# Product 5 by inner products in both chunks of the last gated layer, product 6 in the last one

## The chip, the cores and the metric

The kernel runs on one core of a Trainium2 chip. The metric is the device time of one execution in microseconds, given as the median of repeated runs. A profile of one further execution belongs to it. In the profile PE is TensorE (the matmuls), PEld its loading of weights, DVE VectorE, ACT ScalarE, POOL GpSimd and SP SyncE; here SP issues nearly all transfers.

## The reference

Four layers with residuals, A, B, A, B, on x of 2048 tokens by D = 1024, with F = 3584:

```python
x = x + A(layernorm(x));  x = x + B(layernorm(x))
x = x + A(layernorm(x));  x = x + B(layernorm(x))

def A(x):   # linear attention, 32 heads of 32
    q, k, v = heads(x @ wqkv)
    pq, pk = phi(q), phi(k)          # t + 1 if t > 0 else exp(t), + 1e-6
    kv = einsum("bhsd,bhse->bhde", pk, v);  z = pk summed over s
    return heads_joined((pq @ kv) / (pq . z + 1e-6)) @ wo

def B(x):   # gated, with ReLU
    gate, up = x @ W_gate, x @ W_up          # 1024 x 3584 each
    return (relu(gate) * up) @ W_down
```

The layers are called 0 to 3; layers 1 and 3 are gated. The change lies in these: product 5 and product 6 below are parts of `x @ W_gate` and `x @ W_up`.

## The kernel before

A gated layer works on two chunks c of 1024 tokens; (3, 1) is the second chunk of layer 3. In a chunk `glu` runs over 14 units u of 256 columns of F. In a unit gate ("g") and up ("u") are each a product of 1024 tokens x 1024 by 1024 x 256, cut into 2 x 2 blocks and multiplied by Strassen's scheme in Winograd's form: seven products m = 1 to 7. Each product is one group of four matmuls, 128 x 128 weights by 512 tokens, so a plain unit has 14 groups. The weights come from a ring of tiles. A tile of the ring holds, for one matrix and one unit, the raw weights and four sums of weight blocks, called T; product 5 uses T[0], product 7 T[1], product 6 T[2] and product 4 T[3]. The sums are made in (1, 0), stored in DRAM (`tgu`), and loaded with the raw weights from then on (`load_gu`: two transfers of 512 KB for each matrix and unit). The token side has its own sums s1 to s4, made once for each chunk.

The result of product 5 is V. In a unit the groups follow one another as 5, 1 for g and u, then 2, 6 for g and u, then 7, 3 and 4. An eviction copies X (product 1) to Y on ACT, Z = Y + V is made on VectorE (`zg`, `zu`, line 1300), V = Y + V after product 7 (line 1320), and `put` multiplies by the ReLU of the gate on VectorE (line 1275) into h. TensorE's groups of a unit are all at line 1259.

In (3, 1), from u = 2 on, product 5 is not computed in the unit. For two units together (a pair: the same token blocks, both matrices, two units of weights) it is made by a second level of the same scheme: `inner_gi` has seven steps (five, one, two, six, seven, three, four), each one group of four matmuls of 256 columns (line 1094), in two PSUM banks of their own. The steps run in the odd unit before the pair, each after one of the unit's groups; after which is written by hand in `INNER_AT`, counted in groups. The results are 128 x 512 tiles laid in memory that x has left (`gi_v`), two pairs deep. The weight side of the inner products is made in (3, 0): `make_gi` loads T[0] of four units again from DRAM, makes four sums for each pair on VectorE (line 1072), and stores seven blocks of each pair in DRAM (`gi`); `load_gi` brings the seven blocks of a pair to (3, 1). Because of this, `load_gu` leaves out T[0] of these units.

What sets the order: every engine runs its instructions in the order of issue. `later.at(n, f)` issues f after n more groups of TensorE; `behind(self.last_put, ...)` places work on VectorE after the last `put`. SP's queue carries loads of the ring, of the pairs, the stores of sums, the transposes of activations, and rows of x that are sent to DRAM (`send_away`) and brought back (`bring_back`), because the memory is full. `make_dd` makes and stores the sums of one product of `down`, which follows the 14 units of a chunk. A ring tile can be loaded again when the unit that used it is done; the ring is five tiles deep, and layer_B asks for the tiles up to five ahead at a unit's start. A tile of "big" (16 slots) is also the home of h, of the ring, and of scratch.

Of the kernel before, what the change touches and what calls it, by code (L numbers as in the profile page):

```python
# [8 lines left out]
ALU = mybir.AluOpType  # L9
# [3 lines left out]
F16 = mybir.dt.float16  # L13
PSUM = bass.MemoryType.PSUM
P = 128
# [77 lines left out]
class _Net:  # L93
    def __init__(self, tc, ctx, x_d, wqkv_d, wo_d, wg_d, wu_d, wd_d, out_d):
# [36 lines left out]
        self.dd = {p: self.spill.tile([P, 7, self.U // 2, NW // 2], F16, name=f"dd{p}") for p in self.DEEP}  # L131
        self.gi = [self.spill.tile([P, 7, 2, 2, P], F16, name=f"gi{p}") for p in range(self.U // 2)]
        self.later = _Later()
# [838 lines left out]
    def plan_B(self, l):  # L972
        for c in range(2):
            for u in range(self.U):
                for w in "gu":
                    self.ring.add((l, c, w, u), lambda t, w=w, u=u, first=(l == 1 and c == 0),
                                  lo=(l, c) == (3, 1) and u > 1: self.load_gu(t, w, u, first, lo))
# [70 lines left out]

    GI_AT = (0, 3, 5), (1, 4, 2, 6)

    def make_gi(self, pairs, at):

        def load():
            t = self.slot(f"gi{pairs[0]}", [P, 2, 2, 2, 4, P], F16)
            for i, p in enumerate(pairs):
                for a in range(2):
                    for n, w in enumerate("gu"):
                        self.nc.sync.dma_start(out=t[:, i, n, a, :, :].rearrange("p k f -> p (k f)"),
                                               in_=self.tgu[w, 2 * p + a][:, 0, :])
            self.gi_b = [[[t[:, i, :, a, 2 * j:2 * j + 2, :] for a in range(2)] for j in range(2)]  # L1060
                         for i in range(2)]
            self.later.at(4, lambda: [store(i, m, self.gi_b[i][j][a]) for i in range(2)
                                      for m, j, a in ((0, 0, 0), (3, 1, 0), (5, 1, 1))])

        def store(i, m, b):
            for n in range(2):
                self.nc.sync.dma_start(out=self.gi[pairs[i]][:, m, n, :, :], in_=b[:, n, :, :])

        def sums(i, n):
            (b11, b12), (b21, b22) = self.gi_b[i]  # L1070
            out, a, b, m = ((b11, b12, b11, 1), (b12, b22, b12, 4), (b22, b22, b11, 2), (b21, b21, b22, 6))[n]
            self.nc.vector.tensor_tensor(out=out, in0=a, in1=b, op=ALU.subtract)
            self.later.at(2, lambda: store(i, m, out))

        self.later.at(at, load)
        for i in range(2):
            for n in range(4):
                self.later.at(at + 12 + 2 * (4 * i + n), lambda i=i, n=n: self.behind(
                    self.last_put, lambda n: sums(i, n), (n,)))

    def inner_gi(self, p):

        nc, v = self.nc, self.nc.vector
        H, V, A = NW // 2, self.gi_v[p % 2], self.gi_a
        B = {m: self.gi_w[:, n] for n, m in enumerate((1, 5, 6, 2, 7, 3, 4))}
        out = lambda i, a: V[:, a, :, i, :]
# [3 lines left out]

        def mm(m, b, start=False):
            for w in range(2):
                for k in range(2):
                    nc.tensor.matmul(b[:, w, :], lhsT=B[m][:, w, k, :], rhs=A[m][:, k, :],
                                     start=start and w == 0 and k == 0, stop=k == 1, skip_group_check=True)

        def five():
            z = bank(0)
            mm(5, z, True)
            copy(out(1, 1), z)  # L1100

# [9 lines left out]
        def six():  # L1111
            mm(6, S["y"])
            S["z"] = bank(0)
            v.tensor_tensor(out=S["z"], in0=S["y"], in1=out(1, 1), op=ALU.add)

        def seven():
            mm(7, S["y"])
            v.tensor_tensor(out=out(1, 1), in0=S["y"], in1=out(1, 1), op=ALU.add)

# [9 lines left out]

    def ready_gi(self):  # L1130

        flat = lambda t: self.xall[:, t:t + 2, :].rearrange("p a n -> p (a n)")
        H = NW // 2
        self.gi_w = flat(0).bitcast(F16)[:, 0:28 * P].rearrange("p (m w k f) -> p m w k f", m=7, w=2, f=P)
        self.gi_v = [flat(t).rearrange("p (a w i n) -> p a w i n", a=2, w=2, n=H) for t in (2, 4)]
        S1, S2, S3, S4 = (self.x[6].bitcast(F16)[:, n * NW:(n + 1) * NW].rearrange("p (k n) -> p k n", n=H)
                          for n in range(4))
        s1 = self.xs[3, 1][0]
        (a11, a12), (a21, a22) = ([s1[:, 2 * j:2 * j + 2, i * H:(i + 1) * H] for j in range(2)] for i in range(2))
        v = self.nc.vector  # L1140
        v.tensor_tensor(out=S1, in0=a21, in1=a22, op=ALU.add)
        v.tensor_tensor(out=S2, in0=S1, in1=a11, op=ALU.subtract)
        v.tensor_tensor(out=S3, in0=a11, in1=a21, op=ALU.subtract)
        v.tensor_tensor(out=S4, in0=a12, in1=S2, op=ALU.subtract)
        self.gi_a = {1: a11, 2: a12, 3: S4, 4: a22, 5: S1, 6: S2, 7: S3}

    def load_gi(self, p):
        self.nc.sync.dma_start(out=self.gi_w, in_=self.gi[p])

    def raw_gu(self, t):  # L1150
# [4 lines left out]

    def load_gu(self, t, w, u, first, lo):
        self.nc.sync.dma_start(out=self.raw_gu(t),
                               in_=self.wgu_v[w][:, :, u * 2 * P:(u + 1) * 2 * P])
        if not first:
            self.nc.sync.dma_start(out=t[:, 4 + lo:8, :].bitcast(F16), in_=self.tgu[w, u][:, lo:4, :])  # L1160

# [79 lines left out]

    INNER_AT = (0, 2, 3, 5, 7, 9, 11)

    def glu(self, l, c, u, hT):
# [12 lines left out]
        def mm(w, m, ps, start=False):  # L1257
            for k in range(4):
                nc.tensor.matmul(ps, lhsT=W[w][m][:, k, :], rhs=A[m][:, k, :],  # L1259
                                 start=start and k == 0, stop=k == 3, skip_group_check=True)  # L1260
            if inner and next(turn) in self.INNER_AT:
                inner.pop(0)()
            later.tick()

        deep = (l, c) == (3, 1)
        inner = self.inner_gi(u // 2 + 1) if deep and u % 2 and u + 1 < self.U else []
        turn = count(0 if u > 1 else -2)
        h = hT[u // 2][:, (u % 2) * 4:(u % 2) * 4 + 4, :]
# [14 lines left out]
        def one(w):  # L1283
            X[w] = self.ps.tile([P, NW], F32, tag="a", name=f"x{w}")
            mm(w, 1, X[w], True)
            Y[w] = self.ps3.tile([P, NW], F32, tag="b", name=f"y{w}")
            nc.scalar.activation(out=Y[w], in_=X[w], func=ACT.Copy)

# [8 lines left out]
        def six(w):  # L1297
            mm(w, 6, Y[w])
            Z[w] = self.ps.tile([P, NW], F32, tag="a", name=f"z{w}")
            self.last_z = nc.vector.tensor_tensor(out=Z[w], in0=Y[w], in1=V[w], op=ALU.add)  # L1300

        if c == 0 and u == 0:
            for f in (one, two, five, six):
                for w in "gu":
                    f(w)
        elif deep and u > 1:
            for k, w in enumerate("gu"):
                V[w] = self.gi_v[u // 2 % 2][:, u % 2, k, :, :].rearrange("p i n -> p (i n)")
            for f in ((one,), (two, six)):
# [8 lines left out]
        for w in "gu":  # L1318
            mm(w, 7, Y[w])
            nc.vector.tensor_tensor(out=V[w], in0=Y[w], in1=V[w], op=ALU.add)  # L1320
            if w == "g":
# [17 lines left out]
    def down(self, l, c, hT, final):  # L1339
# [214 lines left out]
        else:  # L1554
            product("T3", raw(2), Y, False, third_done)
            product("T4", raw(3), Y, False, last_done)

    def layer_B(self, l, final):
        ring = self.ring
# [5 lines left out]
        for c in range(2):  # L1565
# [3 lines left out]
            for u in range(self.U):  # L1569
# [26 lines left out]
                if (l, c) == (3, 0) and u in (3, 7, 9):  # L1596
                    self.make_gi({3: (1, 2), 7: (3, 4), 9: (5, 6)}[u], 1)
                if (l, c, u) == (3, 1, 0):
                    self.later.at(4, lambda: behind(self.last_put, self.ready_gi))
                if (l, c) == (3, 1) and u % 2 == 0 and u + 2 < self.U:  # L1600
                    self.later.at(5 if u == 0 else 1, lambda u=u: self.load_gi(u // 2 + 1))
                if (l, c, u) in ((1, 1, 6), (3, 0, 4)):
                    self.make_dd("T4" if l == 1 else "21", 1)
# [76 lines left out]
```

## Time and profile before

| | us |
|---|---|
| median of 3 runs | 1445.16 |
| lowest and highest | 1445.1 and 1445.32 |
| the profiled execution's own time | 1445.22 |
| its span, first to last instruction | 1443.4 |
| TensorE busy in the span | 1436.3 |
| VectorE, ACT, POOL busy | 980.0, 615.7, 308.7 |

The span is what the trace shows; about 1.8 us of the execution's time lie around it. A busy matmul row counts overlapping instructions, so the time from one start to the next start tells what a matmul costs, not its length. Where the stages lie in the span (us): units of (1, 1) from 479.1 to 646.4, of (3, 0) from 930.9 to 1112.4, of (3, 1) from 1194 to 1360.4.

### The profile page before, as it was taken

How to read it: one execution, taken by the hardware profiler on the slowest of the kernel's cores; microseconds unless marked ns; L12 is line 12 of the kernel's file. 1: busy time of each engine (PE TensorE's matmuls, PEld its weight loads, DVE VectorE, ACT ScalarE, POOL GpSimd, SP SyncE). 2: the span in 40 equal slices, each digit the busy share in tenths (PEclk: the TensorE clock that was granted, in tenths of full speed). 3: DMA queues.
4: the chain of work that ended last, by engine and by line, in shares of the span. 5: the costliest groups of instructions: out<-in, count | busy, mean ns of one | idle time of the engine just before them, and what ended most of it. 6: DMA issues, size and time to landing. Idle time of an engine off the chain costs nothing.

```text
span 1443.4 us, 20611 instructions
## 1 busy us (share of the span) xinstructions
PE 1436.3 (100%) x7502; PEld 716.7 (50%) x7502; DVE 980.0 (68%) x1839; ACT 615.7 (43%) x1119; POOL 308.7 (21%) x221
## 2 busy tenths in 40 slices
PE   9999999999999999999999999999999999999998
PEld 4444444444455444445654444444444565555457
DVE  7978698677594456539778885765555864444695
ACT  7872564233334234332068626633333433444300
POOL 1453861011100011110031576410111011111102
PEclk9999999999999999999999999999999999999999
DMA  9950787898469999646983119978976698655465
GB/s 285 240 161 8 175 212 203 287 328 264 164 202 299 352 300 311 201 134 208 292 268 95 59 30 256 266 229 248 306 242 215 213 308 260 206 183 175 153 235 181
DMA packets 345253, 315.93 MB, mean 219 GB/s; under 512 B 109280, under 2 KB 307424, under 8 KB 344128
## 3 DMA queue, kind: packets, MB, share of 16 engines
q1 hardware_dynamic: 337104, 293.32, 68.3%
q10 hardware_dynamic: 6560, 17.24, 3.2%
q0 software_dynamic: 1488, 4.07, 0.8%
q8 instruction: 58, 0.95, 0.3%
q14 instruction: 43, 0.35, 0.1%
HBM read 232.78 MB, written 57.15 MB: 201 GB/s over the span
## 4 chain that ended last, share of the span: by engine, by line
PE 94%; DVE 4%; ACT 1%; issue 1%; DVEq 0%; ACTq 0%
PE ps L495 11%; PE yu L1259 10%; PE yg L1259 10%; PE dy L1384 8%; PE xg L1259 6%; PE xu L1259 6%; PE dx L1384 6%; PE ps L778 4%; PE zu L1259 3%; PE zg L1259 3%; PE my L577 3%; PE vu L1259 3%; PE vg L1259 3%; PE dyT L1436 2%; PE mv L577 2%; PE mx L577 2%
## 5 line engine op out<-in xcount | busy, mean ns | idle before, releaser
L1259 PEld LDWEIGHTS <-w 128*128 128x128 f16 (+1 forms) x3040 | 297.3, 98 | 352.6 <-issue 3.9
L1324 POOL TENSOR_TENSOR h<-m5u,m5g 128x512 f16<-128x512 f32 x44 | 56.6, 1286 | 594.7 <-DVE m5u L1320 555.5
L495 PE MATMUL ps<-w,xnT 128*128 128x512 bf16 x768 | 170.0, 379 | 0.2 <-DVE pq L441 0.2
L1300 DVE TENSOR_TENSOR zg<-yg,m5g 128x512 f32<-128x512 f32 x44 | 30.7, 699 | 130.7 <-PE yg L1259 126.8
L495 PEld LDWEIGHTS <-xnT 128*128 128x128 bf16 x768 | 74.4, 98 | 90.0 <-issue 1.8
L1259 PE MATMUL yu<-s,w 128*128 128x512 f16 x448 | 114.9, 379 | 0.6 <-DVE zu L1300 0.5
L1259 PE MATMUL xu<-xnT,w 128*128 128x512 f16 x448 | 115.0, 379 | 0.0
L1259 PE MATMUL xg<-xnT,w 128*128 128x512 f16 x448 | 114.9, 379 | 0.0
L1259 PE MATMUL yg<-s,w 128*128 128x512 f16 x448 | 114.9, 379 | 0.0
L1384 PEld LDWEIGHTS <-h 128*128 128x128 f16 x672 | 65.8, 98 | 78.2
L1436 PEld LDWEIGHTS <-h 128*128 128x128 f16 x966 | 94.5, 98 | 12.3
L438 ACT ACTIVATE e<-e,eps 128x512 f32<-128x512 f32 x128 | 91.0, 720 | 3.2
L725 POOL TENSOR_TENSOR kvc<-pq,kvc 128x1024 f32<-128x1024 bf16 x32 | 78.5, 2454 | 53.1 <-DVE den L730 32.8
L1384 PE MATMUL dx<-w,h 128*128 128x512 bf16 x392 | 85.3, 379 | 0.0
L778 PE MATMUL ps<-T,pqT 128*128 128x512 bf16 x384 | 83.6, 379 | 0.0
L1275 DVE TENSOR_TENSOR h<-yu,r 128x512 f16<-128x512 f32 x56 | 38.7, 691 | 52.0 <-PE yu L1259 52.0
L516 POOL TENSOR_TENSOR kvc<-kvc,slab 128x512 f32<-128x512 f32 x46 | 57.2, 1249 | 76.0 <-DVE slab L441 72.7
L1272 ACT ACTIVATE r<-zg 128x512 f32<-128x512 f32 x56 | 32.8, 586 | 84.3 <-PE zg L1259 84.3
L1281 ACT ACTIVATE m5g<-vg 128x512 f32<-128x512 f32 x44 | 26.3, 597 | 95.2 <-PE vg L1259 95.2
L437 ACT ACTIVATE e<-ps 128x512 f32<-128x512 f32 x92 | 54.3, 590 | 28.7 <-PE ps L495 28.1
L1272 ACT ACTIVATE r<-yg 128x512 f32<-128x512 f32 x56 | 33.4, 597 | 75.8 <-PE yg L1259 75.8
L737 POOL TENSOR_TENSOR pq<-pq,den 128x1024 bf16<-128x1024 bf16 x32 | 61.2, 1911 | 6.8 <-DVE den L732 5.0
(252 smaller groups left out, 2446.1 us busy)
## 6 DMA issues: line engine op xcount, KB each, us to landing
w<-in_B_W_gate_dram SPq DMA_DIRECT2D x56, 512.0 KB, 6.4
w<-in_B_W_up_dram SPq DMA_DIRECT2D x56, 512.0 KB, 6.0
w<-ddT SPq DMA_DIRECT2D x21, 896.0 KB, 6.4
w<-td SPq DMA_DIRECT2D x18, 896.0 KB, 5.2
w<-tg SPq DMA_DIRECT2D x30, 512.0 KB, 7.3
w<-tu SPq DMA_DIRECT2D x30, 512.0 KB, 6.6
w<-dd SPq DMA_DIRECT2D x15, 896.0 KB, 5.0
w<-in_B_W_down_dram SPq DMA_DIRECT2D x14, 896.0 KB, 4.8
```

The costliest lines, as they stand in the source:

```text
L438: self.last_exp = nc.scalar.activation(out=e, in_=e, func=ACT.Exp, scale=-1.0, bias=self.eps6[:, 0:1])
L495: nc.tensor.matmul(by_row(ps), lhsT=self.xnT[l, l_q][:, kt, j * P:(j + 1) * P], rhs=w[:, kt, :].rearrange("p (b i d) -> p i b d", i=R, d=H ...
L516: nc.gpsimd.tensor_tensor(out=ksum[:, cols], in0=ksum[:, cols], in1=pk, op=ALU.add)
L577: nc.tensor.matmul(banks[j], lhsT=A(i)[:, j * P:(j + 1) * P], rhs=B(i), start=start and i == 0, stop=i == NS - 1, skip_group_check=True)
L725: nc.gpsimd.tensor_tensor(out=prod, in0=pq_of[sc, j], in1=zrow, op=ALU.mult)
L737: nc.gpsimd.tensor_tensor(out=heads(pq), in0=heads(pq), in1=den[:, :].unsqueeze(2).to_broadcast([P, D // HD, HD]), op=ALU.mult)
L778: nc.tensor.matmul(ps, lhsT=pqT[sc][:, g, j * P:(j + 1) * P], rhs=T[g // 4][:, g % 4, n2 * NW:(n2 + 1) * NW], start=(g == 0), stop=(g == G ...
L1259: nc.tensor.matmul(ps, lhsT=W[w][m][:, k, :], rhs=A[m][:, k, :], start=start and k == 0, stop=k == 3, skip_group_check=True)
L1272: self.last_relu = nc.scalar.activation(out=out, in_=ps, func=ACT.Relu)
L1324: nc.gpsimd.tensor_tensor(out=h[:, 3, :], in0=V["u"], in1=V["g"], op=ALU.mult)
L1384: nc.tensor.matmul(banks[j], lhsT=A(k)[:, j * P:(j + 1) * P], rhs=w[:, i, :], start=start and k == 0, stop=k == self.U - 1, skip_group_che ...
L1436: nc.tensor.matmul(bank[:, j * H:(j + 1) * H], lhsT=A[i // 2][:, i % 2, j * P:(j + 1) * P], rhs=B[m][:, i, :], start=start and i == 0 and ...
```

## The change

Which products are made by inner products is now a table, `INNER`, and inner steps can be made for two products at a time.

- Product 5 in (3, 0): units 4 to 13 (five pairs), as in (3, 1). Product 6 in (3, 1): units 3 to 12 (five pairs); the steps of product 6's pairs run in the even unit before the pair, those of product 5 in the odd one.
- Where product 6 is made, its group is left out of the unit, and Y = X + V6 is an add on VectorE in the place of ACT's copy.
- `make_gi` no longer reads T from DRAM again. It takes the T blocks out of the ring's tiles as they pass: T[0] in (1, 1), at even u from 2 to 12, with its scratch in the part of h that is written later; T[2] in (3, 0), at odd u from 3 to 11, with a scratch "gs" of its own. For each pair there are eight sums of 128x256 on VectorE (in the place of four of 128x512), and five stores.
- V of the inner products is one pair deep instead of two, with step five's result and V after product 7 in temporaries.
- `load_gu` leaves out the T blocks of made products: T[0] in (3, 0) from u = 4, T[0] and T[2] in (3, 1) where both are made.
- Four rows of x (8 to 11) are sent away in unit 0 of (3, 0) and brought back from unit 12 on, because their memory holds V, weights and token sums of the inner products meanwhile. `make_dd("21")` moves from unit 4 to unit 5.

In TensorE's order there are ten more pairs, each with 28 narrow matmuls more and 16 wide ones less; all else is in the same order.

```diff
+    INNER = {(3, 0): {5: range(4, 14)}, (3, 1): {5: range(2, 14), 6: range(3, 13)}}
+    T_GU = {5: 0, 6: 2}
...
+    def make_gi(self, l, c, m, u, at, out):
+        O = out.rearrange("p (n w k f) -> p n w k f", n=4, w=2, f=P)
+        gi = self.gi[m, u]
+        def block(w, a):
+            return self.sums_gu(self.ring.get((l, c, w, u + a)))[:, self.T_GU[m]]
+        def sums(n, w):
+            b1, b2 = (block(w, a) for a in range(2))
+            (b11, b21), (b12, b22) = ([b[:, 2 * j:2 * j + 2, :] for j in range(2)] for b in (b1, b2))
+            for o, a, b in ((0, b12, b11), (2, b22, b12), (1, b22, O[:, 0, n]), (3, b21, O[:, 1, n])):
+                self.nc.vector.tensor_tensor(out=O[:, o, n], in0=a, in1=b, op=ALU.subtract)
+        for n, w in enumerate("gu"):
+            self.later.at(at + n, lambda n=n, w=w: self.nc.sync.dma_start(
+                out=gi[:, 4:6, n, :, :], in_=block(w, 0).rearrange("p (j k) f -> p j k f", j=2)))
+            self.later.at(at + 2 + 2 * n, lambda n=n, w=w: self.behind(self.last_put, lambda n: sums(n, w), (n,)))
+            self.later.at(at + 4 + n, lambda n=n, w=w: self.nc.sync.dma_start(
+                out=gi[:, 6, n, :, :], in_=block(w, 1)[:, 2:4, :]))
+        self.later.at(at + 6, lambda: self.nc.sync.dma_start(out=gi[:, 0:4, :, :, :], in_=O))
...
-    def load_gu(self, t, w, u, first, lo):
+    def load_gu(self, t, w, u, first, d):
...
-            self.nc.sync.dma_start(out=t[:, 4 + lo:8, :].bitcast(F16), in_=self.tgu[w, u][:, lo:4, :])
+            b = slice(1, 4, 2) if 6 in d else slice(5 in d, 4)
+            self.nc.sync.dma_start(out=t[:, 4:8, :][:, b, :].bitcast(F16), in_=self.tgu[w, u][:, b, :])
...
-    INNER_AT = (0, 2, 3, 5, 7, 9, 11)
+    INNER_AT = {(5, 12): (0, 2, 4, 6, 9, 10, 11), (5, 10): (1, 2, 3, 5, 7, 8, 9), (6, 10): (1, 2, 4, 5, 7, 8, 9)}
...
+        made = self.is_inner(l, c, u)
+        inner, at, turn = [], (), None
+        for m, us in self.INNER.get((l, c), {}).items():
+            if u + 1 in us and (u + 1 - us[0]) % 2 == 0:
+                steps = 14 - 2 * len(made)
+                n = min(steps, 12 if m == 5 else 10)
+                inner, at, turn = self.inner_gi(m), self.INNER_AT[m, n], count(n - steps)
...
+            if 6 in made:
+                nc.vector.tensor_tensor(out=Y[w], in0=X[w], in1=V6[w], op=ALU.add)
+                return
             nc.scalar.activation(out=Y[w], in_=X[w], func=ACT.Copy)
...
-            mm(w, 6, Y[w])
+            if 6 not in made:
+                mm(w, 6, Y[w])
...
+    def plan_inner(self, l, c, u, hT):
+        at = self.later.at
+        ready = lambda m, *homes: self.behind(self.last_put, lambda m: self.ready_gi(l, c, m, *homes), (m,))
+        if (l, c) == (1, 1):
+            if u % 2 == 0 and u > 1:
+                self.make_gi(l, c, 5, u, 2, hT[u // 2][:, 4:8, :].rearrange("p a n -> p (a n)"))
+        if (l, c) == (3, 0):
+            if u == 0:
+                for n in range(4):
+                    at(1 + 2 * n, lambda t=self.NS + n: self.send_away(t))
+            if u == 2:
+                self.inner_s = self.slot("gs", [P, 8 * NW], F16)
+                at(6, lambda: ready(5, 10, 8, self.inner_s[:, 0:4 * NW]))
+            if u % 2 and 2 < u < self.U - 1:
+                self.make_gi(l, c, 6, u, 2, self.inner_s[:, 4 * NW:8 * NW])
+            if u == self.U - 2:
+                for t in range(2, 4):
+                    at(t, lambda t=t: self.bring_back(self.NS + t))
+        if (l, c) == (3, 1):
+            if u == 0:
+                at(4, lambda: ready(5, 0, 2, 6))
+            if u == 1:
+                at(4, lambda: ready(6, self.slot("gw", [P, 32 * P], F16), 4, 7))
+        for m, us in self.INNER.get((l, c), {}).items():
+            if u + 2 in us and (u + 2 - us[0]) % 2 == 0:
+                at(7 if u + 2 == us[0] else 1, lambda m=m: self.load_gi(m, u + 2))
...
-                if (l, c, u) in ((1, 1, 6), (3, 0, 4)):
+                self.plan_inner(l, c, u, hT)
+                if (l, c, u) in ((1, 1, 6), (3, 0, 5)):
                     self.make_dd("T4" if l == 1 else "21", 1)
...
+            for n in range(2 if (l, c) == (3, 0) else 0):
+                self.later.at(2 + n, lambda t=n + self.NS: self.bring_back(t))
```

More of the change, by code (lines that the diff above doesn't have):

```diff
@@ L131, in __init__ @@
         self.dd = {p: self.spill.tile([P, 7, self.U // 2, NW // 2], F16, name=f"dd{p}") for p in self.DEEP}
-        self.gi = [self.spill.tile([P, 7, 2, 2, P], F16, name=f"gi{p}") for p in range(self.U // 2)]
+        self.gi = {(m, u): self.spill.tile([P, 7, 2, 2, P], F16, name=f"gi{m}_{u}")
+                   for m, first in ((5, 2), (6, 3)) for u in range(first, self.U - 1, 2)}
+        self.inner = {}
         self.later = _Later()
@@ L976, in plan_B @@
                     self.ring.add((l, c, w, u), lambda t, w=w, u=u, first=(l == 1 and c == 0),
-                                  lo=(l, c) == (3, 1) and u > 1: self.load_gu(t, w, u, first, lo))
+                                  d=self.is_inner(l, c, u): self.load_gu(t, w, u, first, d))
             for p in self.order_d(l, c):
@@ L1047, in make_dd @@
             self.later.at(at + 18 + 4 * n, lambda n=n: self.behind(self.last_put, lambda n: self.sums_dd(p, n), (n,)))
[L1049 to L1079, printed above, removed]
@@ L1081, in inner_gi, with is_inner, rows @@
-    def inner_gi(self, p):
+    INNER = {(3, 0): {5: range(4, 14)}, (3, 1): {5: range(2, 14), 6: range(3, 13)}}
+    T_GU = {5: 0, 6: 2}
+    def is_inner(self, l, c, u):
+        return [m for m, us in self.INNER.get((l, c), {}).items() if u in us]
+    def rows(self, t):
+        return self.xall[:, t:t + 2, :].rearrange("p a n -> p (a n)")
+    def make_gi(self, l, c, m, u, at, out):
[15 more added lines that the diff above has]
+        self.later.at(at + 6, lambda: self.nc.sync.dma_start(out=gi[:, 0:4, :, :, :], in_=O))
@@ new lines, in ready_gi @@
+    def ready_gi(self, l, c, m, wt, vt, st):
+        H = NW // 2
+        wt = self.rows(wt) if isinstance(wt, int) else wt
+        w = wt.bitcast(F16)[:, 0:28 * P].rearrange("p (m w k f) -> p m w k f", m=7, w=2, f=P)
+        V = self.rows(vt).rearrange("p (a w i n) -> p a w i n", a=2, w=2, n=H)
+        st = self.x[st] if isinstance(st, int) else st
+        S1, S2, S3, S4 = (st.bitcast(F16)[:, n * NW:(n + 1) * NW].rearrange("p (k n) -> p k n", n=H)
+                          for n in range(4))
+        s = self.xs[l, c][{5: 0, 6: 1}[m]]
+        (a11, a12), (a21, a22) = ([s[:, 2 * j:2 * j + 2, i * H:(i + 1) * H] for j in range(2)] for i in range(2))
+        v = self.nc.vector
+        v.tensor_tensor(out=S1, in0=a21, in1=a22, op=ALU.add)
+        v.tensor_tensor(out=S2, in0=S1, in1=a11, op=ALU.subtract)
+        v.tensor_tensor(out=S3, in0=a11, in1=a21, op=ALU.subtract)
+        v.tensor_tensor(out=S4, in0=a12, in1=S2, op=ALU.subtract)
+        self.inner[m] = w, V, {1: a11, 2: a12, 3: S4, 4: a22, 5: S1, 6: S2, 7: S3}
@@ L1083, in inner_gi, with load_gi @@
+    def load_gi(self, m, u):
+        self.nc.sync.dma_start(out=self.inner[m][0], in_=self.gi[m, u])
+    def inner_gi(self, m):
         nc, v = self.nc, self.nc.vector
-        H, V, A = NW // 2, self.gi_v[p % 2], self.gi_a
-        B = {m: self.gi_w[:, n] for n, m in enumerate((1, 5, 6, 2, 7, 3, 4))}
+        H = NW // 2
+        weights, V, A = self.inner[m]
+        B = {k: weights[:, n] for n, k in enumerate((5, 6, 7, 4, 1, 2, 3))}
         out = lambda i, a: V[:, a, :, i, :]
@@ L1089, in inner_gi, with mm @@
         S = {}
-        def mm(m, b, start=False):
+        def mm(p, b, start=False):
             for w in range(2):
                 for k in range(2):
-                    nc.tensor.matmul(b[:, w, :], lhsT=B[m][:, w, k, :], rhs=A[m][:, k, :],
+                    nc.tensor.matmul(b[:, w, :], lhsT=B[p][:, w, k, :], rhs=A[p][:, k, :],
                                      start=start and w == 0 and k == 0, stop=k == 1, skip_group_check=True)
@@ L1099, in five @@
             mm(5, z, True)
-            copy(out(1, 1), z)
+            S["5"] = self.temp([P, 2, H], name="i5")
+            copy(S["5"], z)
         def one():
@@ L1113, in six @@
             S["z"] = bank(0)
-            v.tensor_tensor(out=S["z"], in0=S["y"], in1=out(1, 1), op=ALU.add)
+            v.tensor_tensor(out=S["z"], in0=S["y"], in1=S["5"], op=ALU.add)
         def seven():
             mm(7, S["y"])
-            v.tensor_tensor(out=out(1, 1), in0=S["y"], in1=out(1, 1), op=ALU.add)
+            v.tensor_tensor(out=out(1, 1), in0=S["y"], in1=S["5"], op=ALU.add)
         def three():
@@ L1128, in inner_gi @@
         return [five, one, two, six, seven, three, four]
[L1130 to L1148, printed above, removed]
     def raw_gu(self, t):
@@ L1260, in mm @@
                                  start=start and k == 0, stop=k == 3, skip_group_check=True)
-            if inner and next(turn) in self.INNER_AT:
+            if inner and next(turn) in at:
                 inner.pop(0)()
             later.tick()
-        deep = (l, c) == (3, 1)
-        inner = self.inner_gi(u // 2 + 1) if deep and u % 2 and u + 1 < self.U else []
-        turn = count(0 if u > 1 else -2)
+        made = self.is_inner(l, c, u)
[5 more added lines that the diff above has]
+                inner, at, turn = self.inner_gi(m), self.INNER_AT[m, n], count(n - steps)
+        for m in made:
+            a = (u - self.INNER[l, c][m][0]) % 2
+            VI = {w: self.inner[m][1][:, a, k, :, :].rearrange("p i n -> p (i n)") for k, w in enumerate("gu")}
+            if m == 5:
+                V5 = VI
+            else:
+                V6 = VI
         h = hT[u // 2][:, (u % 2) * 4:(u % 2) * 4 + 4, :]
@@ L1305, in glu @@
                     f(w)
-        elif deep and u > 1:
-            for k, w in enumerate("gu"):
-                V[w] = self.gi_v[u // 2 % 2][:, u % 2, k, :, :].rearrange("p i n -> p (i n)")
+        elif 5 in made:
+            V.update(V5)
             for f in ((one,), (two, six)):
@@ L1319, in glu @@
             mm(w, 7, Y[w])
-            nc.vector.tensor_tensor(out=V[w], in0=Y[w], in1=V[w], op=ALU.add)
+            m5, V[w] = V[w], self.temp(name=f"c22{w}") if 5 in made else V[w]
+            nc.vector.tensor_tensor(out=V[w], in0=Y[w], in1=m5, op=ALU.add)
             if w == "g":
@@ L1595, in layer_B @@
                                 self.last_put, lambda: self.sums_w(w, n)))
[L1596 to L1601, printed above, removed]
-                if (l, c, u) in ((1, 1, 6), (3, 0, 4)):
+                self.plan_inner(l, c, u, hT)
+                if (l, c, u) in ((1, 1, 6), (3, 0, 5)):
                     self.make_dd("T4" if l == 1 else "21", 1)
```

## The prediction

> **What bounds the kernel now.** I read the page's rows by engine first, then the chain that ended last, then TensorE's timeline inside the stage that the change touches, and last the windows for what the other engines have free there.
>
> ```profile
> PE 1436.3 (100%) x7502; PEld 716.7 (50%) x7502; DVE 980.0 (68%) x1839; ACT 615.7 (43%) x1119; POOL 308.7 (21%) x221
> ...
> PEclk9999999999999999999999999999999999999999
> DMA  9950787898469999646983119978976698655465
> ...
> PE 94%; DVE 4%; ACT 1%; issue 1%; DVEq 0%; ACTq 0%
> ```
>
> TensorE is busy 1436.3 of 1443.4 us at full clock, and 94% of the chain is TensorE. A change gains only by taking TensorE time away, and loses only where TensorE then waits. So I need the price of a matmul of either width, and the places where a wait can appear. From the chain of waits (start, length, line, count):
>
> ```profile
> 1112.59 24.17 PE dx L1384 x112
> 1136.77 1.53 PE dxT L1436 x14
> ```
>
> 112 matmuls of 512 columns in 24.17 us are 215.9 ns each; 14 of 256 columns in 1.53 us are 109.1 ns each. From the timeline of TensorE at the end of unit 2 and in unit 3 of (3,1), where the kernel before already works by inner products (start, length, line):
>
> ```profile
> 1230.65 1.03 PE L1259 MATMUL xg<-xnT,w 128*128 128x512 f16 x4
> 1231.52 0.60 PE L1094 MATMUL i<-x 128*128 128x256 f16 x4
> 1231.95 1.03 PE L1259 MATMUL xu<-xnT,w 128*128 128x512 f16 x4
> ...
> 1245.03 1.03 PE L1259 MATMUL xu<-xnT,w 128*128 128x512 f16 x4
> 1245.92 1.02 PE L1259 MATMUL xg<-xnT,w 128*128 128x512 f16 x4
> ...
> 1254.55 1.03 PE L1259 MATMUL xg<-xnT,w 128*128 128x512 f16 x4
> ...
> 1258.91 0.60 PE L1094 MATMUL i<-s,x 128*128 128x256 f16 x4
> ```
>
> The lengths overlap; starts count. A group of four wide matmuls steps on by 0.864, a group of four narrow ones by 0.436 (1231.52 to 1231.95). The second xg starts 0.89 after xu, not 0.864: a wait of 0.03.
>
> **The change part by part.**
>
> 1. *Matmuls.* For a pair of units, one product of both matrices is 2 x 2 x 4 = 16 wide matmuls, 16 x 215.9 = 3.454 us. By inner products it is 7 groups of four narrow ones, 7 x 0.4355 = 3.049. A pair gains 0.405. Pairs go from 6 to 16 (five more of product 5 in (3,0), five of product 6 in (3,1)): 10 x 0.405 = 4.05 us.
>
> Here a rule of the Trainium skill speaks against the change. "TensorE: Matmul & The Clock Gate", section "Back-to-back issue gap", gives for a sustained stream of weight loads and matmuls some 81 ns at 128 columns and 131 ns at 512, and calls N/2.4 + 2.5 ns the isolated gap. Between its two sustained points 256 columns come to about 98 ns (my estimate from that page): a pair would cost 28 x 98 = 2.74 against 16 x 131 = 2.10, a loss of 0.65, over ten pairs 6.5 us slower. The trace has 215.9 and 109.1 in streams that have a weight load for every matmul, and these are the isolated figures of the page. I use the trace: +4.05.
>
> 2. *Waits inside the pairs.* Two units of (3,1) with a pair take 1254.55 − 1230.65 = 23.90 now; two plain units of (3,0) take 24.18 (12.09 each). The gain seen is 0.28, and up to 0.34 in the others: some 0.065 per pair is lost to two waits of 0.03, one at the inner group that follows too soon on a copy (1258.91), one at the second xg of an even unit. The new positions of the inner steps put wide work in these places. In (3,0) the even units keep their 0.03: 5 x 0.405 − 0.15 = 1.87. In (3,1) the six old pairs give back 6 x 0.065 = 0.39. New there: some 0.03 in five units and in units 2 and 13, 0.21 together; and unit 12 has no inner steps left that could cover. With product 6 made, Y = X + V6 is an add on VectorE (0.70, where ACT's copy took 0.58), so yg is done at 1.12 + 0.70 = 1.82 after the unit's start, while its second xg group could start at 1.73, and yu, behind zg's add in VectorE's order, at about 3.16 while the second xu could start at 2.74: together 0.63 lost. So (3,1): 2.02 + 0.39 − 0.21 − 0.63 = 1.57. Sum 3.44.
>
> 3. *Work off TensorE.* VectorE's 24 sums of 0.508 are taken out of (3,0) (five pairs of 8 smaller ones come in), and six pairs of 8 sums of 128x256 come into (1,1), at 0.29 each alone and some 0.22 in a row (the first row below). The rows of VectorE's groups by shape for an add of this size and for the sums that go, then the windows of (1,1) chunk 1, of units 1 to 2 and 4 to 13 of (3,0), and of (3,1):
>
> ```profile
> L1411 DVE TENSOR_TENSOR h<-h 128x256 f16<-128x256 f16 x28 | 8.2, 293 | 0.0
> ...
> L1072 DVE TENSOR_TENSOR gi<-gi 128x512 f16<-128x512 f16 x24 | 11.8, 508 | 1.4 <-DMA gi<-gi 1.3
> ```
>
> ```profile
> 479.10:646.40 167.30, 167.25 (x773) 75.48 (x772) 88.54 (x136) 65.79 (x119) 16.51 (x13) 1.00 0.81 262
> 943.00:968.00 25.00, 25.00 (x117) 11.30 (x116) 16.83 (x23) 9.46 (x17) 2.54 (x2) 1.00 0.61 200
> 979.40:1112.40 133.00, 133.00 (x617) 60.28 (x616) 68.51 (x109) 51.40 (x88) 13.97 (x11) 1.00 0.80 251
> 1194.00:1360.40 166.40, 166.40 (x854) 83.30 (x852) 76.42 (x113) 67.61 (x118) 18.48 (x15) 1.00 0.60 189
> ```
>
> (After the clock column 1.00: DMA share, GB/s.) VectorE is half used in all of them: the sums cost nothing as long as they run when they are placed. ACT's added copies and VectorE's added adds (a few per pair, 0.6 to 0.7 each) lie inside the same free half. That cover goes where the first sum waits for a transfer: VectorE runs in order, and zg or zu, which TensorE needs, stand behind it.
>
>  - (3,0), unit 7: the sums for product 6 stand between xu's product and zu. They read the T blocks of unit 8's weights, whose load can be issued only when a ring tile comes free, about 0.6 before the unit's start; the page's T loads take 6.4 us and more, in this stage 5.2. The sums can start near +4.8 to +6.8, the move of make_dd from unit 4 to 5 puts one 1.08 sum next to them, and zu is wanted at +8.66. From 0 to 1.7; I take 0.2, since most of that span fits. In units 3, 5, 9 and 11 the load is issued earlier: nothing (3 and 11 bounded by 0 to 0.5).
>  - (1,1), even units: the sums need the T blocks of the next unit at about +3.5 to +4.7. In the trace these loads were issued before the even unit started: w(u,3) at 496.10 for unit 2 at 503.43, w(u,5) at 519.92 for unit 4 at 527.76, and landed in 5 to 10 us. They just fit. But each pair adds five stores, 0.9 MB, some 2.7 us of the queues at the 340 GB/s seen there while they are full (until about 575). SP issues in order, so the stores also stand ahead of later weight loads. From 0 to 3 together; I take 0.2, since the loads have a unit's lead and the adds before were hidden.
>  - (3,0), unit 0: four sends of 512 KB of x stand between the transposes of pqT on SP's queue, in a stretch in which the DMA is full. pqT feeds the sums of T, and behind these stands zg (948.85). They start at 944.07 and may start some 4 us later before TensorE waits. 2 MB are about 6 us of transfers, shared with the loads. From 0 to 2; I take 0.3. The returns at unit 12 and after it meet queues with the last loads only, and are wanted in the next chunk's down products: nothing.
>  - Loads of made weights in (3,0) and (3,1) (896 KB, 4.7 us) are issued a unit ahead; the left-out T blocks take 0.13 to 0.25 MB away per load, in smaller pieces: nothing, −0.2 to +0.5.
>
> *Sum:* 3.44 − 0.7 = 2.7 us off the profiled execution's 1445.22 (1443.4 span and 1.8 around it), which lies 0.06 above the median: 1442.5.
>
> **The rivals.** What this kernel can tell from no change is about 0.2%, 2.9 us, so that the likeliest case stands at that line.
>
>  - *All waits stay covered* (chance 0.25). VectorE at half load and a unit's lead of the weights speak for it; the gain is 3.2 to 3.7: 1441.5 to 1442.
>  - *Small waits, as summed* (0.45). 2.0 to 3.3 off: 1441.9 to 1443.2.
>  - *More of them* (0.15): unit 7 and the unit 0 of (3,0) at their upper ends, 2 to 3 us lost: 1443.2 to 1445.
>  - *VectorE is held in (1,1)* (0.13): slower. If the stores push the T loads so that they land later than about +4.7 in the even unit (over 11 to 12 us from issue instead of 5 to 10), the sums hold zg and TensorE waits, and since each pair delays the next loads too, it repeats: at 1 to 2 us in six pairs, 6 to 12 lost against 3.4 gained, 1448 to 1454. For it: the DMA share there is 0.98 to 1.06 in most units to 575. Against: TensorE waits for no transfer there now, and from 590 on the queues are half empty, so that two of six pairs can't suffer.
>  - *The narrow stream doesn't keep 109 ns* (0.02): the page's sustained figures, +6.5, as in part 1. Against it stand 168 narrow inner matmuls in this very trace.
>
> **How the numbers follow.** Predicted 1442.5. Faster by over 0.2% (below 1442.3): the first case and four tenths of the second, 0.25 + 0.20 = 0.45. Within: the rest of the second and most of the third, 0.38. Slower: the fourth and fifth and a tail of the third, 0.17. The range 1441.2 to 1446.0 leaves out the slower cases (0.15) and a small tail below.
>
> **What would show it.** Narrow inner groups go from 42 to 112 (7 per pair) at 0.436 each; two units of (3,0) from unit 4 on step 23.75 to 23.80 instead of 24.18; (3,1) with a product 6 pair 23.45 to 23.55. VectorE's idle before the new sums would name the DMA of w in unit 7 of (3,0) if I am right there. A wait of TensorE on zg in an even unit of (1,1), or unit steps above 12.3 there, would show the slower rival. Pair steps that don't shrink would refute the main term.

## The result and the profile after

The changed kernel takes 1442.26 us, median of 14 runs (1441.49 to 1443.22), against 1445.22 for the kernel before in 14 runs beside it. The ratio is 0.9979, 95% interval 0.9971 to 0.9987: 2.96 us less. The forecast was 1442.5, in a range of 1441.2 to 1446.0. The profiled execution took 1442.3 us with a span of 1440.5, so again 1.8 lie around the span, and it is at the median. The runs of the changed kernel are spread more widely: without the three lowest and the three highest of 14 they span 1442.01 to 1442.80, those of before 1445.09 to 1445.52.

From the page of the changed kernel: the row by engines (busy time, share, instructions) and the first lines of the chain that ended last.

```profile
PE 1431.3 (99%) x7592; PEld 728.0 (51%) x7622; DVE 1014.4 (70%) x1951; ACT 619.1 (43%) x1129; POOL 309.9 (22%) x221
...
PE 93%; DVE 4%; ACT 1%; issue 1%; DMA 0%; DVEq 0%; SPq 0%; ACTq 0%
```

TensorE still carries the chain, at 93% where it was 94%, and DMA and SPq have come into it with shares that round to nothing. One of these small pieces is a load of 7.00 us at 573.39 (`w<-tu`), and it is there that part of the gain was lost. Below, the two traces are laid against each other stage by stage, by the start of the first matmul group behind each boundary. (In the trace before, the units of (1,1) end at 649.16 and those of (3,1) begin at 1193.00.)

| stage | before, us | after, us | difference |
|---|---|---|---|
| up to unit 1 of (1,1) | 491.18 | 491.00 | −0.18 |
| (1,1), units 1 to 13 | 157.98 | 158.91 | +0.93 |
| from there to unit 1 of (3,0) | 294.03 | 293.99 | −0.04 |
| (3,0), units 1 and 2 | 24.82 | 24.83 | +0.01 |
| (3,0), from the products of layer 2 that follow unit 2 to down | 144.42 | 142.58 | −1.84 |
| down of (3,0) and unit 0 of (3,1) | 92.66 | 92.66 | 0.00 |
| (3,1), units 1 to 13 | 155.19 | 153.37 | −1.82 |
| the rest | 83.12 | 83.16 | +0.04 |

The sum is −2.90, the difference of the two spans. A unit's step, in what follows, is the time from its start to the start of the next unit. TensorE's timeline at the starts of two pairs of units in (3,0):

```profile
1029.51 1.03 PE L1264 MATMUL xg<-xnT,w 128*128 128x512 f16 x4
1030.38 0.60 PE L1117 MATMUL i<-gs,x 128*128 128x256 f16 x4
...
1053.32 1.03 PE L1264 MATMUL xg<-xnT,w 128*128 128x512 f16 x4
```

Two units now take 53.32 − 29.51 = 23.81 us, where two plain ones took 24.18: 0.37 for a pair.

The loss is in unit 8 of (1,1), where nothing was removed from TensorE: it steps 13.02 instead of 12.11. TensorE before, then TensorE, VectorE, ACT and SP of the changed kernel there (start, length, line, in brackets the idle time before and who ended it):

```profile
580.93 1.03 PE L1259 MATMUL yg<-s,w 128*128 128x512 f16 x4
581.79 1.03 PE L1259 MATMUL xu<-xnT,w 128*128 128x512 f16 x4
```

```profile
579.90 1.03 PE L1264 MATMUL xg<-xnT,w 128*128 128x512 f16 x4
580.76 1.03 PE L1264 MATMUL yg<-s,w 128*128 128x512 f16 x4
582.30 1.02 PE L1264 MATMUL xu<-xnT,w 128*128 128x512 f16 x4 [0.51 <-ACT yu L1306]
583.16 1.03 PE L1264 MATMUL yu<-s,w 128*128 128x512 f16 x4
584.24 1.02 PE L1264 MATMUL yg<-s,w 128*128 128x512 f16 x4
```

```profile
571.26 1.08 DVE L1042 TENSOR_TENSOR ddT<-ddT,ddT 128x1792 f16<-128x1792 f16 x1
...
579.12 0.28 DVE L1072 TENSOR_TENSOR h<-w,h 128x256 f16<-128x256 f16 x1
580.41 0.29 DVE L1072 TENSOR_TENSOR h<-w,w 128x256 f16<-128x256 f16 x1 [1.01 <-DMA w<-tu]
...
581.23 0.20 DVE L198 BATCH_NORM_AGGREGATE mv<-stats 128x2 f32<-128x12 f32 x1
...
583.50 0.68 DVE L1320 TENSOR_TENSOR zg<-yg,m5g 128x512 f32<-128x512 f32 x1
```

```profile
581.47 0.29 ACT L176 ACTIVATE rstd<-mv,eps 128x1 f32<-128x1 f32 x1 [1.63 <-DVE mv L198]
581.67 0.58 ACT L1306 ACTIVATE yu<-xu 128x512 f32<-128x512 f32 x1
```

```profile
567.23 5.50 SPq L1033 DMA_DIRECT2D ddT<-ddT  x2
572.83 0.52 SPq L1161 DMA_DIRECT2D w<-in_B_W_up_dram  x1
573.39 1.22 SPq L1165 DMA_DIRECT2D w<-tu  x1
```

Read from the bottom: SP's queue is at two ddT stores from 567.23 to 572.73. The second of them waits for a sum that VectorE makes from 571.26 to 572.34 (4.6 us of waiting), and only then comes the load of unit 9's T blocks. In the kernel before, this second store stood behind the load:

```profile
566.32 0.36 SPq L1031 DMA_DIRECT2D ddT<-ddT  x1
...
567.33 2.30 SPq L1160 DMA_DIRECT2D w<-tu  x1
572.53 0.36 SPq L1031 DMA_DIRECT2D ddT<-ddT  x1
```

So the load went out 9.3 us ahead of unit 8 then, and goes out 3.1 ahead of it now. Why the new instructions changed this order is not shown. (TensorE's zg group of unit 7, for which the load could have waited too, accounts for 0.2 us at most, and in the kernel before the load went out ahead of that group.)

From there on upwards: the T blocks are there at 580.41, 3.96 into unit 8. VectorE's sum has waited 1.01 for them. Behind it stands mv, a step of the next layer's norm; on ACT rstd waits for mv, and behind rstd stands yu, the copy that TensorE's second xu group needs. xu starts 1.54 after yg instead of 0.864: 0.68 lost. zg, which comes at 583.50, costs 0.22 more at the next yg. So one late transfer passes through VectorE and ACT before it reaches TensorE.

### The profile page after: what moved, and what is told of

Read it like the earlier page. It is cut to its first block, busy times and chain, and to the rows that moved or that the text cites. A ratio compares the mean times of both kernels' runs of the same rounds, so it can differ in the third digit from the quotient of the medians.

```text
span 1440.5 us, 20916 instructions
## 1 busy us (share of the span) xinstructions
PE 1431.3 (99%) x7592; PEld 728.0 (51%) x7622; DVE 1014.4 (70%) x1951; ACT 619.1 (43%) x1129; POOL 309.9 (22%) x221
## 4 chain that ended last, share of the span: by engine, by line
PE 93%; DVE 4%; ACT 1%; issue 1%; DMA 0%; DVEq 0%; SPq 0%; ACTq 0%
PE ps L497 11%; PE yu L1264 9%; PE yg L1264 9%; PE dy L1404 8%; PE xg L1264 6%; PE xu L1264 6%; PE dx L1404 6%; PE ps L780 4%; PE i L1117 3%; PE zg L1264 3%; PE zu L1264 3%; PE my L579 3%; PE dyT L1456 2%; PE vu L1264 2%; PE mv L579 2%; PE mx L579 2%
## 5 line engine op out<-in xcount | busy, mean ns | idle before, releaser
L1264 PEld LDWEIGHTS <-w 128*128 128x128 f16 (+1 forms) x2880 | 281.4, 98 | 320.0 <-issue 5.2
L1344 POOL TENSOR_TENSOR h<-m5u,m5g 128x512 f16<-128x512 f32 x34 | 44.7, 1316 | 487.8 <-DVE m5u L1340 376.9
L1264 PE MATMUL yu<-s,w 128*128 128x512 f16 x408 | 104.7, 379 | 0.6 <-DVE zu L1320 0.5
L1264 PE MATMUL yg<-s,w 128*128 128x512 f16 x408 | 104.9, 379 | 0.1
L1456 PEld LDWEIGHTS <-h 128*128 128x128 f16 x966 | 94.5, 98 | 12.4
L1320 DVE TENSOR_TENSOR zg<-yg,m5g 128x512 f32<-128x512 f32 x34 | 23.7, 698 | 84.4 <-PE yg L1264 80.5
L1344 POOL TENSOR_TENSOR h<-c22u,c22g 128x512 f16<-128x512 f32 x22 | 28.0, 1271 | 229.0 <-DVE c22u L1340 197.2
```

The lines of the kernel that those rows point to most:

```text
L1344: nc.gpsimd.tensor_tensor(out=h[:, 3, :], in0=V["u"], in1=V["g"], op=ALU.mult)
L1456: nc.tensor.matmul(bank[:, j * H:(j + 1) * H], lhsT=A[i // 2][:, i % 2, j * P:(j + 1) * P], rhs=B[m][:, i, :], start=start and i == 0 and ...
```

## The experiments

**Sums of one pair later.** In unit 8 of (1,1) alone:

```diff
-                self.make_gi(l, c, 5, u, 2, hT[u // 2]...)
+                self.make_gi(l, c, 5, u, 4 if u == 8 else 2, hT[u // 2]...)
```

> The changed kernel with the sums for product 5 of units 8 and 9 in (1,1) (their scratch store too) placed two groups later, in unit 8 alone; all else as changed. Theory (VectorE is held by the landing of w<-tu at 580.41, ACT's rstd and yu wait behind it, TensorE loses 0.91 in unit 8): the sums then come after the landing, unit 8 steps 12.1 to 12.2 instead of 13.02, the time falls by 0.9 to about 1441.4. Also the spread of the changed kernel's runs (1441.5 to 1443.2) shrinks towards that of before (0.3), if the landing is what varies. Rival (VectorE simply has more work in unit 8 than fits, 11.3 of 12.4 us were busy before): the sums cost the same later, unit 8 still steps 12.8 to 13.0, the time stays at 1442.3.

In the trace unit 8 went from 576.78 to 589.10, 12.32 instead of 13.02. The median was 1442.29 (9 runs, 1441.7 to 1444.29; ratio 0.9977, 0.9968 to 0.9987), neither lower nor less spread than the changed kernel's. So the trace seems to take the side of the theory, but it doesn't show that the edit did it. In this execution the load took 6.4 us to land instead of 7.0, and with that unit 8 would step about 12.4 in the unchanged kernel as well (an estimate from the table below): the edit itself brought about 0.1. VectorE has little room there in either order: zg came at 583.11, behind further steps of the norm, and the next yg group lost 0.16.

**The changed kernel once more**, on the chip of the runs with another start of make_dd, with doubled stores and with both remedies.

> The changed kernel as it is, on the same chip as the three that follow. Both theories: 1442.3, within 0.5; unit 8 of (1,1) steps between 12.1 and 13.3, differing from one execution to the next, while the stages (3,0) from unit 3 on and (3,1) keep their steps within 0.05.

The median was 1442.16 (11 runs, 1441.71 to 1443.35; ratio 0.9979, 0.997 to 0.9988). In the profiled execution, the longest of them at 1443.35, unit 8 stepped 12.12: T had landed in time. From the products to down, (3,0) took 142.59, and (3,1) 153.38. The time had gone elsewhere, to the down stage of (1,1), whose instructions the change leaves alone, and where its loads queue with transposes. TensorE's timeline of this run:

```profile
699.16 0.39 PE L1404 MATMUL dy<-w,h 128*128 128x512 f16 x1 [1.00 <-DMA w<-td]
```

A second wait, of 0.57, stood at 1188.35 behind VectorE. So the spread of the changed kernel has more than one source, and unit 8 is one. How much it loses is told by five traces together: the two of the changed kernel and those of the three kernels further down whose edits lie in layer 3. In all five, TensorE, VectorE, ACT and SP run their instructions of (1,1) in the same order, and the load of unit 9's T goes out 3.05 or 3.06 ahead of unit 8.

| kernel | the load, issue to landing, us | step of unit 8, us |
|---|---|---|
| product 6 alone | 5.9 | 12.09 |
| the changed kernel, second trace | 6.1 | 12.12 |
| product 5 alone | 6.5 | 12.57 |
| the changed kernel, first trace | 7.0 | 13.02 |
| step two later | 7.2 | 13.24 |

Up to about 6.1 us the landing costs next to nothing, and beyond it each tenth of landing is a tenth of TensorE's time. So it is the landing that varies from one execution to the next, and the landing that sets the loss.

**Another start of make_dd.** In (1,1) two units later, so that no ddT store stands ahead of unit 9's loads:

```diff
-                if (l, c, u) in ((1, 1, 6), (3, 0, 5)):
+                if (l, c, u) in ((1, 1, 8), (3, 0, 5)):
```

> The changed kernel with make_dd of T4 in (1,1) begun in unit 8 instead of 6. Theory (in unit 8 the T load of unit 9 is late because SP's queue stands from 567.23 to 572.8 behind a ddT store that waits for VectorE): the loads of unit 9 are issued some 4 to 6 us earlier, VectorE doesn't wait for w<-tu, unit 8 steps 12.1, the median falls by 0.4 to 0.9 against the unchanged kernel of the same chip. Rival (the load is late because the DMA is full there, not because of the queue): unit 8 still waits, the median stays.

The median was 1441.59 (11 runs, from 1441.29; eight at or under 1442.32, three from 1442.78 to 1443.71; ratio 0.9977, 0.9968 to 0.9986), 0.57 under the unchanged kernel of the same chip. By the medians alone the two can't be told apart, since three of eleven runs lie above 1442.7 in either. The trace tells more. SP's queue and TensorE in this run:

```profile
558.04 1.93 SPq L1165 DMA_DIRECT2D w<-tu  x1
```

```profile
580.78 1.03 PE L1264 MATMUL yg<-s,w 128*128 128x512 f16 x4
581.64 1.03 PE L1264 MATMUL xu<-xnT,w 128*128 128x512 f16 x4
```

The load that was issued at 573.39 now goes out at 558.04, 15 us earlier where 4 to 6 were expected, xu follows yg by 0.86, and unit 8 steps 12.09. Unit 7, at 12.29 before and after the change, steps 12.08 as well; dd's sums have left it. The rival, a DMA that is too full, is answered by the same load: it took 9.2 us to land, longer than in any of the five traces above, and the wait was gone, because it was issued 18 us ahead of unit 8. So the place in SP's queue decides. The edit moves more than this load, though: ACT's rstd no longer stands ahead of yu in unit 8 either. The five traces in one order are the cleaner evidence for the path, this run for the queue.

**Every store of (1,1)'s pairs twice**, the second to another place in DRAM:

```diff
-        self.later.at(at + 6, lambda: self.nc.sync.dma_start(out=gi[:, 0:4, :, :, :], in_=O))
+        self.later.at(at + 6, lambda: [self.nc.sync.dma_start(out=g[:, 0:4, :, :, :], in_=O) for g in gis])
...
```

Here gis holds both places.

> The changed kernel with every store of product 5's pairs in (1,1) issued a second time, to another place in DRAM: 0.9 MB more per pair, all else the same. It prices the rival of the prediction that ended slower. Theory (the queues there are full, so that T lands later, VectorE is held in more units): some units of (1,1) from 4 to 9 step 0.5 to 2.5 longer, in all 1 to 4 us more than the unchanged kernel: 1443.5 to 1446. Rival (a unit's lead of the loads takes it): steps as in the unchanged kernel, 1442.3 within 0.3.

The median was 1443.62 (11 runs; ratio 0.9989, 0.998 to 0.9997), 1.46 above the unchanged kernel of the same chip, at the low end of what was expected. In the trace the loss came in units 4 (12.95 instead of 12.25) and 8 (12.79). Unit 4 on VectorE and TensorE:

```profile
533.68 0.29 DVE L1073 TENSOR_TENSOR h<-w,w 128x256 f16<-128x256 f16 x1 [2.58 <-DMA w<-tu]
...
534.29 0.69 DVE L1321 TENSOR_TENSOR zg<-yg,m5g 128x512 f32<-128x512 f32 x1
...
536.82 0.69 DVE L1321 TENSOR_TENSOR zu<-yu,m5u 128x512 f32<-128x512 f32 x1
```

```profile
535.90 1.03 PE L1265 MATMUL zg<-s,w 128*128 128x512 f16 x4
537.57 1.02 PE L1265 MATMUL yu<-s,w 128*128 128x512 f16 x4 [0.65 <-DVE zu L1321]
```

In unit 4 this is the slower rival: the T blocks land 5.61 into the unit (528.07 to 533.68), past the 4.7 from which it was to decide, VectorE stands for 2.58, zg and zu are late, and TensorE loses 0.70. But the load did not take longer, as the rival had it (over 11 us from issue). It took 8.9 us, and 9.1 in the changed kernel; it was issued later, at 524.75 where the changed kernel issued it at 521.80, behind twice the stores of the first pair. So this too is the queue's order of issue rather than the landing.

Unit 8 lost its 0.70 in another way. The kernel with the doubled stores did not keep all else the same: in units 6 to 8 TensorE's order is another than in the changed kernel, and so are those of VectorE, ACT and SP. In unit 8, ACT and TensorE:

```profile
582.22 0.60 ACT L1298 ACTIVATE m5u<-vu 128x512 f32<-128x512 f32 x1 [1.98 <-PE vu L1265]
```

```profile
583.56 1.02 PE L1265 MATMUL xu<-xnT,w 128*128 128x512 f16 x4 [0.52 <-ACT yu L1307]
```

The group vu now stands behind the second xg, ACT's copy of it stands ahead of the copy yu, and xu waits for yu. The sums of the pair come at 588.92, behind all this, and hold nothing. So only unit 4's 0.70 is the price of the rival; the rest of the 1.46 is not shown to be.

**Product 5 alone.** Product 6's pairs taken out of table and planner:

```diff
-    INNER = {(3, 0): {5: range(4, 14)}, (3, 1): {5: range(2, 14), 6: range(3, 13)}}
+    INNER = {(3, 0): {5: range(4, 14)}, (3, 1): {5: range(2, 14)}}
```

> The changed kernel without product 6's pairs (neither their sums in (3,0) nor their steps in (3,1)); product 5 by pairs in both chunks, weights from the ring's tiles. Theory (each part gains by TensorE's count alone, (3,0) 1.84 and (3,1) 1.82, less 0.9 in unit 8 of (1,1)): (3,0) keeps its 1.84, (3,1) loses 5 x 0.405 = 2.02 less the waits that product 6 brings (some 0.5) and lies 0.2 to 0.4 under before by the new positions, the wait in (1,1) stays; about 1443.8. Rival (the parts lean on each other, the sums in (3,0) hold something): (3,0) is faster here than 1.84 by more than 0.3.

The median was 1443.58 (11 runs; before on this chip 1445.38; ratio 0.9985, 0.9976 to 0.9994), close to the 1443.8 expected. In its trace (3,0) took 142.59 from the products to down, the 142.58 of the changed kernel; (3,1) took 154.93, 0.26 under before, which is what the new positions of the steps give to the six old pairs. So product 6's five pairs bring 154.93 − 153.37 = 1.56, or 0.31 each.

**Product 6 alone.** Product 5's pairs in (3,0) taken out, with the sends of x and their returns:

```diff
-    INNER = {(3, 0): {5: range(4, 14)}, (3, 1): {5: range(2, 14), 6: range(3, 13)}}
+    INNER = {(3, 1): {5: range(2, 14), 6: range(3, 13)}}
...
-                for n in range(4):
-                    at(1 + 2 * n, lambda t=self.NS + n: self.send_away(t))
```

> The changed kernel without product 5's pairs in (3,0) (no sends of x, no loads of pairs there); product 5 and 6 by pairs in (3,1), all sums from the ring's tiles, the sums for ten units in (1,1) made but used only in (3,1). Theory: (3,1) gains 1.82, (3,0) 0, unit 8 of (1,1) loses 0.9: about 1444.2 to 1444.4. The start of (3,0) is the same without the four sends of x (they were hidden). Rival (the sends cost at the start of (3,0), prediction 0.3): the start of (3,0) up to unit 3 is 0.3 shorter.

The median was 1444.14 (11 runs; ratio 0.9991, 0.9982 to 1.0: by the runs alone it is barely told from no change). In the trace (3,1) took 153.38 and the stretch from unit 1 of (3,0) to the products 24.82, as with the sends (24.83). From the end of (1,1) to unit 1 of (3,0) it took 294.00; with the sends 293.99. The sends were hidden: 0 instead of the 0.3 that I took. Against before on their chip the two parts alone bring 1.80 and 1.24; each carries the sums in (1,1) of which one set is needed, and both have the new positions.

**Step two later.** In (3,1) a wait was left in every second unit. TensorE and ACT in unit 9 of the changed kernel:

```profile
1306.00 0.60 PE L1117 MATMUL i<-s,x 128*128 128x256 f16 x4
1306.44 1.03 PE L1264 MATMUL xu<-xnT,w 128*128 128x512 f16 x4
1307.40 0.60 PE L1117 MATMUL i<-s,x 128*128 128x256 f16 x4
```

```profile
1306.26 0.60 ACT L1288 ACTIVATE r<-xg 128x512 f32<-128x512 f32 x1 [0.33 <-PE xg L1264]
1306.76 0.59 ACT L1110 ACTIVATE i<-i 128x512 f32<-128x512 f32 x1
```

Step two comes 0.96 after xu instead of 0.864, since the copy i that it needs stands on ACT behind the ReLU r. The edit:

```diff
-    INNER_AT = {..., (5, 10): (1, 2, 3, 5, 7, 8, 9), (6, 10): (1, 2, 4, 5, 7, 8, 9)}
+    INNER_AT = {..., (5, 10): (1, 2, 4, 5, 7, 8, 9), (6, 10): (1, 2, 4, 5, 7, 8, 9)}
```

> The changed kernel with the steps of product 5's pairs in units of ten groups after groups 1, 2, 4, 5, 7, 8, 9 instead of 1, 2, 3, 5, 7, 8, 9: step two goes behind the group of product 7. Theory (in five or six odd units of (3,1) step two waits 0.10 for ACT's copy i, which stands behind r<-xg): pairs of units in (3,1) step 23.37 instead of 23.47, the time falls by 0.5 to about 1441.8. Rival (the wait moves on to step six or three, which need adds on VectorE): pairs of units stay at 23.47 or more, the time stays within 0.2 of 1442.3.

In its trace two units of (3,1) with both products step 23.38 (1303.28 to 1326.66) instead of 23.47, and (3,1) takes 152.90 instead of 153.37. The median of 1442.14 (9 runs; ratio 0.9977, 0.9967 to 0.9987) is not the 1441.8 that was expected and doesn't show the gain by itself: in the profiled execution unit 8 of (1,1) stepped 13.24, and down of (1,1) waited 0.57 for w<-td.

**Both remedies together**, step two later and make_dd later:

> Step two of product 5's pairs behind product 7's group (units of ten groups in (3,1)) and make_dd of T4 in (1,1) begun in unit 8, together. If both hold: 0.45 from (3,1), as its trace alone showed, and 0.4 to 0.9 from (1,1): 1441.0 to 1441.5. If the second doesn't: 1441.8.

The median was 1441.73 (7 runs, 1440.88 to 1442.27; ratio 0.9973, 0.9963 to 0.9984), with a profiled execution of 1441.21: unit 8 stepped 12.08, (3,1) took 152.91. It beats the kernel before and lies 0.43 under the changed one in the medians on one chip. It missed the 1441.0 to 1441.5 that was expected if both remedies hold, and is nearer to the 1441.8 written for the case that the second does not. The traces say that both hold; the median doesn't. Against make_dd later alone (1441.59) the medians tell no difference, and that the lowest runs differ by 0.41 (1440.88 against 1441.29), close to what the trace of (3,1) gains, may be chance. I take it for the best version by its trace, not by its median.

## Why the prediction was right

- *The main term held.* Ten pairs, each 0.405 by the starts of groups: TensorE's narrow groups kept their 0.44 (1306.00 to 1306.44). (From the two rounded rows of the chain a pair's gain comes out at 0.39: 24.17/112 is 215.8 ns and 1.53/14 is 109.3.) (3,0) was to bring 1.87 before waits for transfers and brought 1.84, two units 23.81 where 23.75 to 23.80 was written.
- *The sustained gaps of the Trainium skill ("TensorE: Matmul & The Clock Gate", section "Back-to-back issue gap") don't hold here.* By the estimate from them the change would have cost 6.5 us; it brought 2.96, and the trace's 216 and 109 ns made the right sum.
- *(3,1) was near in sum and wrong in two terms.* 1.57 was forecast, 1.82 came. Unit 12 was charged 0.63 for Y's add on VectorE without inner steps as cover. It took 8.71 (1338.24 to 1346.95) for ten groups of 0.864, a loss of 0.07. I had put the second xu straight behind the second xg, but in the trace three matmuls of product 7 stand between (1340.91), and xu starts at 1341.56, when yu's add is done. The other term erred the other way: 0.03 was charged for a waiting unit where step two's place behind a ReLU on ACT costs 0.10, five times. The step that failed is thus the order of evictions on ACT and VectorE inside the new units, not the price of any instruction.
- *Unit 7 of (3,0) was to lose 0.2*, and lost nothing: VectorE waited once in this stage for w<-tu, 0.96 at 974.02, which is ahead of unit 3, and not at all in unit 7.
- *(1,1) was to lose 0.2 with bounds 0 to 3.* In the first trace it lost 0.93, in the other four of the table 0 to 1.15, all in unit 8; "they just fit" was true of the other units. The mechanism was the one named (VectorE in order behind a landing), but the way to TensorE was another: through mv to ACT's rstd and yu first, and only then zg. The point from which it costs was set too late for unit 8: about 3.0 into the unit (6.1 from issue), not 3.5 to 4.7, since VectorE has no free time behind the sums there. And what made the load late was SP's queue behind a store of make_dd, which I had not charged: I read the lead of the loads in units 2 and 4 and took the queue's order elsewhere for unchanged, but one store that waits for VectorE had changed places with the load.
- *The start of (3,0) was to lose 0.3* by the sends, and lost nothing.
- *The slower rival* did not come. With twice the stores one unit of six is hit by it, for 0.70, through a later issue and not through a longer landing.

So −0.7 was charged for waits and about 0.9 came in that trace, all of it in (1,1), while (3,1) gave 0.25 more than forecast. These two errors cancel, and (1,1) loses anything from 0 to 1.15 by the execution: that the total came within 0.3 is in part luck, while the main term is not.

## What to carry to other kernels

When a kernel is bound by TensorE, the saving can be counted from the starts of matmul groups in the trace, if groups of both widths already occur in it: here to 0.03 us in one stage and to 0.25 in the other, where the evictions of new units were part of the count. What is lost again hangs on in-order queues: for each new instruction that waits on a transfer, list what stands behind it on its engine, including small steps of a norm that another engine waits for, and for each load, which waiting store stands ahead of it on the issuing queue. Compare that order before and after the change: it can move where no line of the change names it, as it did here and again with the doubled stores. A wait that comes and goes between executions shows in the spread and in the step of one unit across several traces, before it shows in the median.

## What was not expected of the hardware

The changed kernel differed between its two traced executions in where it waited: unit 8 of (1,1) stepped 13.02 in one and 12.12 in the other, and the load w<-td in down of (1,1) cost nothing in the one and 1.00 in the other, while (3,0) and (3,1) were equal to 0.01 us. The load of unit 9's T took 7.0 us to be there in the execution that waited (573.39 to 580.41) and at most 6.1 (573.58 to 579.70) in the one that did not: 0.9 us in one landing was the whole difference in unit 8.
